# The last ten groups of a first layer's last pass by seven quarter products instead of eight

## The chip, the cores and the metric

The kernel runs on one core of a Trainium2 chip. The metric is device time in microseconds (us) of one execution; three runs of the kernel before were timed, and one more was profiled.

## What is computed

Attention over 4 x 8 heads with a threshold under the row maximum, then two feed-forward layers on 2304 tokens of 512 values. Cut to what matters here:

```
x = attention(q, k, v, tau)                      # 2304 x 512
x = (sigmoid(x @ w_gate) * (x @ w_val)) @ w_out  # first layer, 1536 hidden
h = x @ w2_in                                    # second layer, 2048 hidden
g = where(h >= 1, h, where(h <= -1, 0, (h + 1)**2 / 4))
out = g @ w2_out
```

## The kernel before, in words

The inputs of the layers are held as float32, and each product of two float32 matrices is made of three matmuls of rounded pieces: high times high, high times low, low times high. ScalarE writes the high piece (a copy to the rounded type), VectorE the low one (source minus high). The tiles `win_0` and `win_1` hold the high and the low pieces of the weights in the second layer, `wout_0` to `wout_3` both pieces of output weights, `xflat` and `xmore` those of x, `hh` and `hl` those of the hidden values.

The tokens are taken in three passes of 768 (`T`), each in two halves of 384 (`HT`). The hidden values are taken in groups of 128: 12 groups per pass in the first layer (`NF[0]`), 16 in the second, two at a time, eight pairs per pass (`NQ`).

*First layer.* `hidden` does one group: for each half, `up` (L504) makes the gate and the value, four k blocks times three matmuls of 384 columns each, 48 for a group. ScalarE takes the sigmoid, VectorE multiplies, and both make the pieces of the product. Behind it `down` (L777) adds the group before to six accumulators `y`, 24 matmuls. In the gaps `conversions` (L515) turns the weights of later groups and of the second layer from 64-bit words to float32, in pieces taken eight per group step in the first pass and six later (L879), and stores them in device memory (`saved`). After each two groups of the second layer `w_sums` (L539) makes four differences of their quarters on VectorE and stores them (`tsaved`).

*Second layer.* `pair` (L708) does two groups. Their two weight blocks and two k halves make a 2 x 2 block matrix, the two halves of x and their two k halves another one. Seven products of quarters (`product`, L630: six matmuls of 384 columns, 42 in all) give what eight would give, with sums and differences of quarters of x (`x_sums`) and of the weights (`tsum`) made beforehand, and with sums of the products afterwards: ScalarE copies two of them (`s1`, `u2`), VectorE adds five times from PSUM (L715). Products use two PSUM banks in turn. Behind the products stand the 36 output matmuls of the pair before (`down_pair`).

The weight pieces of the next pair go into the same `win_0` and `win_1`: each region is free when the product that reads it last is done. 512 columns (blocks 0 and 1) serve the first two products, 1024 columns (the differences, from `tsum`) the third to sixth, 256 columns the seventh.

*The order.* Each engine runs its instructions in the order in which they are written. In the second layer everything that is not a product, its copies and its additions goes through a list: `due` enters it with a due time on a written-out scale, a first and a last slot and a cost on VectorE or ScalarE, and `fill` (L669) is called three times per pair and writes what is due and fits. The costs, due times and slots are numbers in the program.

## Time and profile before

| what | us |
|---|---|
| median of three runs | 1105.14 (1104.94 to 1107.15) |
| the profiled execution | 1104.5 |
| its span, first to last instruction | 1102.7 |
| TensorE busy | 1082.9 (98%) |
| VectorE busy | 844.2 (77%) |
| ScalarE busy | 614.8 (56%) |

Attention ends at about 290 us. The first layer's passes run to 707 us, the second layer from there to the end. A busy TensorE is not TensorE at its peak, since matmuls are pipelined: the start of each is what counts.

### The profile page before, as it was taken

What the parts mean: (1) busy time and instruction counts of PE and PEld (TensorE: products, weight loads), DVE (VectorE), ACT (ScalarE), POOL (GpSimd) and SP (SyncE); (2) the same over time, 40 slices, a digit from 0 to 9 for tenths busy, and PEclk for the clock granted to TensorE, in tenths of its full rate; (3) what the DMA queues carried; (4) which work ended last, traced back from release to release, by engine and by line L of the source; (5) the groups of instructions that cost most, each with busy time, mean ns of one, the idle gap of its engine ahead of it and who ended that gap; (6) DMA issues with size and microseconds to landing.
All of it is one profiled execution on the core that took longest, in us unless ns stands there. A gap on an engine that the chain in (4) does not pass through costs nothing.

```text
span 1102.7 us, 18536 instructions
## 1 busy us (share of the span) xinstructions
PE 1082.9 (98%) x6996; PEld 933.3 (85%) x6996; DVE 844.2 (77%) x1489; ACT 614.8 (56%) x1000; POOL 152.7 (14%) x315
## 2 busy tenths in 40 slices
PE   8999999999999999999999999999999999999998
PEld 6666666667899999999999999988898898888887
DVE  7999999997999988767686744576767767776663
ACT  6888888886343444333353322565566655665653
POOL 4556666552000000000000000000000000000000
PEclk9999999999999999999999999999999999999999
DMA  5344344413855566545654342223232423233301
GB/s 157 70 100 79 93 99 100 102 34 103 277 199 179 176 214 218 175 150 175 202 172 151 116 153 77 77 77 125 86 114 75 165 105 115 96 134 115 115 20 58
DMA packets 65146, 139.17 MB, mean 126 GB/s; under 512 B 9616, under 2 KB 35872, under 8 KB 65056
## 3 DMA queue, kind: packets, MB, share of 16 engines
q1 hardware_dynamic: 64912, 137.98, 39.2%
q8 instruction: 55, 0.90, 0.3%
q14 instruction: 35, 0.29, 0.1%
q10 hardware_dynamic: 144, 0.00, 0.0%
HBM read 111.15 MB, written 26.81 MB: 125 GB/s over the span
## 4 chain that ended last, share of the span: by engine, by line
PE 85%; ACT 7%; DVE 5%; issue 3%; POOL 0%; DVEq 0%; POOLq 0%; ACTq 0%
PE y L771 14%; PE pu L636 14%; PE y L789 13%; PE pgv L511 9%; PE pgv L512 9%; PE pgv L513 9%; PE av L338 6%; PE w L253 5%; PE w L306 4%; ACT ex L274 2%; PE w L249 1%; ACT sqs L645 1%; ACT sqs L646 1%; ACT hh L654 1%; DVE s L262 1%
## 5 line engine op out<-in xcount | busy, mean ns | idle before, releaser
L511 PE MATMUL pgv<-xflat,win 128*128 128x384 f32 x560 | 187.9, 336 | 3.0 <-DVE act L571 1.8
L512 PE MATMUL pgv<-xflat,win 128*128 128x384 f32 x560 | 187.9, 335 | 0.0
L513 PE MATMUL pgv<-xflat,win 128*128 128x384 f32 x560 | 187.8, 335 | 0.0
L771 PE MATMUL y<-wout,hh 128*128 128x512 f32 x576 | 184.1, 394 | 0.0
L789 PE MATMUL y<-hh,wout 128*128 128x512 f32 (+1 forms) x576 | 146.5, 336 | 0.0
L771 PEld LDWEIGHTS y<-wout,hh 128*128 128x128 f32 x576 | 108.2, 188 | 24.5
L262 DVE TENSOR_SCALAR_CACHE_REDUCE s<-w,nscale 128x576 f32<-128x576 f32 x144 | 112.2, 812 | 9.7 <-PE w L253 7.6
L571 DVE TENSOR_TENSOR act<-pgv,act 128x384 f32<-128x384 f32 x70 | 38.8, 554 | 105.2 <-PE pgv L513 104.9
L572 ACT ACTIVATE hh<-act 128x384 fp32r<-128x384 f32 x72 | 38.0, 528 | 141.7 <-DVE act L571 141.7
L771 PE MATMUL y<-wout,hl 128*128 128x512 f32 x288 | 113.6, 395 | 0.0
L282 DVE SCALAR_TENSOR_TENSOR p<-s,mx,ex 128x576 f32<-128x576 f32 x144 | 111.6, 807 | 0.0
L511 PEld LDWEIGHTS pgv<-xflat,win 128*128 128x128 f32 x560 | 105.6, 188 | 5.0 <-DVE act L571 2.1
L274 ACT ACTIVATE ex<-s,mx 128x576 f32<-128x576 f32 x144 | 104.3, 766 | 6.3 <-DVE s L262 5.9
L789 PEld LDWEIGHTS y<-hh,wout 128*128 128x128 f32 x576 | 98.1, 188 | 11.3
L512 PEld LDWEIGHTS pgv<-xflat,win 128*128 128x128 f32 x560 | 105.5, 188 | 1.6
L636 PE MATMUL pu<-xflat,win 128*128 128x384 f32 x576 | 105.2, 337 | 1.4 <-DVE sqs L715 1.1
L567 ACT ACTIVATE act<-pgv 128x384 f32<-128x384 f32 x70 | 34.2, 489 | 128.7 <-PE pgv L513 128.6
L513 PEld LDWEIGHTS pgv<-xflat,win 128*128 128x128 f32 x560 | 105.7, 189 | 0.0
L636 PEld LDWEIGHTS pu<-xflat,win 128*128 128x128 f32 x576 | 100.6, 188 | 3.1 <-DVE sqs L715 2.0
L789 PE MATMUL y<-hl,wout 128*128 128x512 f32 (+1 forms) x288 | 97.1, 337 | 0.0
L265 POOL TENSOR_SCALAR mx<-mx,tau_b 128x1 f32<-128x1 f32 x144 | 87.4, 607 | 54.7 <-DVE s L262 54.5
L253 PE MATMUL w<-qk 64*128 64x288 f32 x512 | 88.2, 430 | 2.9 <-DVE s L262 2.9
(153 smaller groups left out, 1866.0 us busy)
## 6 DMA issues: line engine op xcount, KB each, us to landing
words<-in_moe_w_out_dram SPq DMA_DIRECT2D x26, 512.0 KB
wmore<-saved SPq DMA_DIRECT2D x24, 512.0 KB
tsum<-tsaved SPq DMA_DIRECT2D x24, 512.0 KB
w<-saved SPq DMA_DIRECT2D x24, 512.0 KB
w<-saved SPq DMA_DIRECT2D x14, 768.0 KB
words<-in_moe_w_in_dram SPq DMA_DIRECT2D x16, 512.0 KB
saved<-w SPq DMA_DIRECT2D x16, 512.0 KB
wmore<-saved SPq DMA_DIRECT2D x10, 768.0 KB
```

The source lines that it names most:

```text
L253: nc.tensor.matmul(w[:, s, :HS], t[es, 0, u * P : u * P + P], t[es, 1, c], start=True, stop=True)
L262: nc.vector.tensor_scalar(t[:, e], w[:, :, :HS], nscale, None, op0=ALU.mult, op1=ALU.min, accum_out=mx[:, 0, e : e + 1])
L265: nc.gpsimd.tensor_scalar(mx[:, 1, e : e + 1], mx[:, 0, e : e + 1], tau_b, None, op0=ALU.add)
L274: nc.scalar.activation(ex[:, e], t[:, e], AF.Exp, scale=-1.0, bias=mx[:, 0, e : e + 1])
L282: nc.vector.scalar_tensor_tensor(pr[:, e], t[:, e].rearrange("p a b -> p (a b)"), mx[:, 1, e : e + 1], ex[:, e].rearrange("p a b -> p (a b ...
L338: nc.tensor.matmul(av[e * D : e * D + D, :n], vs[p % 3][:, e, c], rt[r][:, e, c] if c < nf else rl[r], start=c == 0, stop=c == nf,)
L511: nc.tensor.matmul(ps, ih[:, i, kk], xh[:, kk, c], start=(kk == 0), stop=False)
L512: nc.tensor.matmul(ps, ih[:, i, kk], xl[:, kk, c], start=False, stop=False)
L513: nc.tensor.matmul(ps, il[:, i, kk], xh[:, kk, c], start=False, stop=(kk == KD - 1))
L636: nc.tensor.matmul(ps[bank], l[:, k], r[:, k], start=bool(new) and k == m == 0, stop=k == HK - 1 and m == 2, skip_group_check=True,)
L771: nc.tensor.matmul(y[b], l[:, ts_], r, start=first and m == 0, stop=last and m == 2)
L789: nc.tensor.matmul(at(y, a, b), l[:, ds_], r[:, c], start=new and m == 0, stop=last and m == 2, skip_group_check=True,)
```

## The change

Ten of the twelve groups in the first layer's last pass are taken by seven products as well. Two groups make two stages: a gate stage (even g: both groups' gates, then their sigmoids) and a value stage (odd g: both groups' values, times the sigmoids, then the pieces). `pair` becomes `stage(g)`: g from 0 to 9 is first layer, from 10 on second layer (q = g - 10). Behind stage 0 stand no output matmuls; behind stages 1 to 9 the 24 of one group each; behind stage 10 the 48 of the last two groups.

The weight differences are made one stage ahead on VectorE (`w_sums` with `due_w`): for the ten stages from the loaded weights, never stored; for the second layer in its first pass, then stored and loaded in its later passes. The conversions take eight pieces per step in both passes and end with the second. The x pieces of the first layer are laid out so that three of the seven operands of the stages are pieces that the ordinary groups had; four are made anew.

```diff
-            def w_sums(j):
-
-                b11, b21, b12, b22 = (w[:, i * HC : (i + 1) * HC] for w in w2s for i in range(2))
...
+            def w_sums(g):
+
+                b11, b21, b12, b22 = quarters(g)
+                t2, t3, t1, t4 = (tsum[:, i * HC : (i + 1) * HC] for i in range(4))
+                q = g - N1
+
+                def step(n, o, a, b):
+                    nc.vector.tensor_tensor(o, a, b, op=ALU.subtract)
+                    if n == 3 and q >= 0:
+                        nc.sync.dma_start(out=tsaved[q], in_=tsum)
...
-            LEN = lambda q: 11 if q == 0 else 15
-            start = lambda q: sum(LEN(i) for i in range(q))
+            lens = [7] + [11] * (N1 - 1) + [15] * (NPASS * NQ + 1)
+            start = lambda g: sum(lens[:g])
...
+            def due_w(g):
+                at = start(g)
+                if g < N1 + NQ:
+                    due(4 * g - 3, 4 * g - 1, [(at - 3 + 0.1 * i, 0.4, 0, True, w) for i, w in enumerate(w_sums(g))])
...
+                if q < 0:
+                    if g % 2 == 0:
+                        sig = lambda x: nc.scalar.activation(x, x, AF.Sigmoid)
+                        due(4 * g + 3, 4 * g + 7, [(at + 0.5 + i, 0, 0.9, True, lambda x=x: sig(x)) for i, x in enumerate(c)])
                     else:
...
+                        for i in range(2):
+                            h = hts[0, NPASS - 1, F0 + 2 * n + i] = h_tiles()
+                            when = ((-3.5, -3.4, -2.9), (-3.3, -2, 0.5))[i]
+                            a, *b = gated_steps(c[i], cs[n][i], h, [at + x for x in when])
+                            due(4 * g + 3, 4 * g + 3, [a])
+                            due(4 * g + 3, 4 * g + 7, b)
...
+            def gated_steps(c, s, h, at):
+
+                return [
+                    (at[0], 0.92, 0, False, lambda: nc.vector.tensor_tensor(c, c, s, op=ALU.mult)),
+                    (at[1], 0, 0.82, False, lambda: nc.scalar.activation(h[0], c, AF.Copy)),
+                    (at[2], 0.92, 0, False, lambda: nc.vector.tensor_tensor(h[1], c, f32(h[0]), op=ALU.subtract)),
+                ]
...
-                ops = 8 if order[s][1] == 0 else 6
...
+                work = itertools.islice(conv, 8)
+                if s == NB - 2:
...
+                elif s == NB - 1:
+                    work = (w[4]() for i in (2, 4, 6) for w in split_steps(0, 0, 0, *x_split(0, i)))
...
+                if s == NB - 1:
+                    due_x(0, (3,))
                     due_w(0)
                     fill(-1, 4.4, 4.4)
...
-            for q in range(NPASS * NQ):
-                pair(q)
...
+            for g in range(N1 + NPASS * NQ):
+                q = g - N1
+                if g % 2 == 0 and g + 2 < N1:
+                    for x in order[NB + g + 2 : NB + g + 4]:
+                        load_step(*x)
...
+                stage(g)
+                if q <= 0 < g:
+                    for x in order[NB - 2 + g : NB - 1 + g] if q else order[-2:]:
+                        down(*x[1:], y)
```

The matmuls on `pgv` (gate and value by `up`) go from 1680 to 1200, those on `pu` (quarter products) from 1008 to 1428; the output matmuls stay 1728. VectorE has 98 instructions more, ScalarE 24.

The three places below are all on VectorE. In the names, `pu` and `pgv` are PSUM banks with products, `act`, `high0` the copies and sums of products, `tsum` the four differences of weights, `win_1` the low and `win_0` the high weight pieces, `w32` and `wmore` loaded weights, `rb`, `raw_1`, `sqs`, `vals` the sums for one group each, `ssum` and `raw_0` sums for x.

First place: inside the last pass of the first layer. Before, one ordinary group step on VectorE:

```order
L571 TENSOR_TENSOR act_7157<-pgv_7159,act_7157 128x384
L192 TENSOR_TENSOR win_1_3510<-w32_0_82,win_1_3510 128x1024
L574 TENSOR_TENSOR hl_7156<-act_7157,hh_7155 128x384
L192 TENSOR_TENSOR wout_2_3512<-w32_0_82,wout_2_3512 128x512
L691 TENSOR_TENSOR xmore_7050<-xall_72,xmore_7050 128x768
L571 TENSOR_TENSOR act_7194<-pgv_7196,act_7194 128x384
L574 TENSOR_TENSOR hl_7156<-act_7194,hh_7155 128x384
```

Now, from the last addition of value stage 3 to the first one of gate stage 4:

```order
L749 TENSOR_TENSOR raw_1_88<-pu_6633,act_6636 128x384
L717 TENSOR_TENSOR wout_3_6159<-wmore_3619,wout_3_6159 128x512
L826 TENSOR_TENSOR rb_73<-rb_73,vals_6161 128x768
L826 TENSOR_TENSOR raw_1_88<-raw_1_88,vals_6161 128x768
L828 TENSOR_TENSOR hl_6693<-rb_73,hh_6692 128x768
L621 TENSOR_TENSOR tsum_6160<-w32_1_83 128x256
L621 TENSOR_TENSOR tsum_6160<-w32_0_82,tsum_6160 128x256
L717 TENSOR_TENSOR win_1_3510<-w32_0_82,win_0_89 128x512
L717 TENSOR_TENSOR win_1_3510<-tsum_6160,win_0_89 128x1024
L749 TENSOR_TENSOR sqs_6162<-pu_6734,act_6735 128x384
```

The low weight piece for the next stage's first product (512 columns) stands behind two multiplications, a low piece of h and two differences, where an ordinary step has two operations on the hidden values and two weight pieces.

Second place: the entry to the stages. Before, from the last ordinary group to the first addition of the first pair:

```order
L571 TENSOR_TENSOR act_7288<-pgv_7290,act_7288 128x384
L574 TENSOR_TENSOR hl_7256<-act_7288,hh_7255 128x384
L691 TENSOR_TENSOR win_1_3510<-wmore_3619,win_0_89 128x512
L691 TENSOR_TENSOR win_1_3510<-tsum_7053,win_0_89 128x1024
L691 TENSOR_TENSOR win_1_3510<-wmore_3619,win_0_89 128x256
L691 TENSOR_TENSOR xflat_86<-xall_72,xflat_86 128x768
L691 TENSOR_TENSOR xflat_86<-ssum_7051,xflat_86 128x768
L715 TENSOR_TENSOR sqs_7055<-pu_7355,act_7356 128x384
```

Now, from the last ordinary group to the first addition of stage 0:

```order
L562 TENSOR_TENSOR act_6303<-pgv_6305,act_6303 128x384
L565 TENSOR_TENSOR hl_6269<-act_6303,hh_6268 128x384
L717 TENSOR_TENSOR xmore_6157<-ssum_6158,xmore_6157 128x768
L717 TENSOR_TENSOR xmore_6157<-raw_0_87,xmore_6157 128x768
L621 TENSOR_TENSOR tsum_6160<-w32_2_84,w32_1_83 128x256
L621 TENSOR_TENSOR tsum_6160<-w32_2_84,tsum_6160 128x256
L621 TENSOR_TENSOR tsum_6160<-w32_2_84 128x256
L621 TENSOR_TENSOR tsum_6160<-w32_1_83,tsum_6160 128x256
L717 TENSOR_TENSOR win_1_3510<-w32_1_83,win_0_89 128x512
L717 TENSOR_TENSOR win_1_3510<-tsum_6160,win_0_89 128x1024
L717 TENSOR_TENSOR win_1_3510<-w32_2_84,win_0_89 128x256
L749 TENSOR_TENSOR sqs_6162<-pu_6376,act_6377 128x384
```

Four differences, which were loaded from memory before, now stand ahead of the first low weight piece.

Third place: the exit. There was no such place before. Now, behind the last addition of stage 9, to the piece behind the first addition of stage 10:

```order
L717 TENSOR_TENSOR wout_0_90<-wmore_3619,wout_0_90 128x512
L717 TENSOR_TENSOR wout_2_3512<-w32_0_82,wout_2_3512 128x512
L717 TENSOR_TENSOR win_1_3510<-w32_1_83,win_0_89 128x512
L717 TENSOR_TENSOR xflat_86<-xall_72,xflat_86 128x768
L826 TENSOR_TENSOR rb_73<-rb_73,sqs_6162 128x768
L826 TENSOR_TENSOR raw_1_88<-raw_1_88,sqs_6162 128x768
L828 TENSOR_TENSOR hl_7276<-rb_73,hh_7275 128x768
L621 TENSOR_TENSOR tsum_6160<-w32_1_83,tsum_6160 128x256
L717 TENSOR_TENSOR xflat_86<-xall_72,xflat_86 128x768
L717 TENSOR_TENSOR win_1_3510<-tsum_6160,win_0_89 128x1024
L749 TENSOR_TENSOR sqs_6162<-pu_7318,act_7319 128x384
L717 TENSOR_TENSOR xmore_6157<-ssum_6158,xmore_6157 128x768
```

The low pieces of x for the second and third product of stage 10 stand behind the multiplications of stage 9.

## Rows read from the trace of the kernel before

**Rows 1.** Busy time by stretch, TensorE to GpSimd, granted clock, DMA share, GB/s.

```profile
200.00:300.00 100.00, 93.24 (x787) 70.88 (x784) 90.02 (x183) 67.54 (x119) 38.35 (x69) 0.98 0.44 129
290.00:440.00 150.00, 150.00 (x865) 143.54 (x864) 137.16 (x179) 64.28 (x115) 0.00 (x0) 1.00 0.59 198
581.89:707.03 125.14, 125.14 (x722) 119.76 (x722) 66.35 (x100) 38.85 (x67) 0.00 (x0) 1.00 0.30 104
707.03:764.57 57.54, 55.33 (x289) 49.99 (x289) 41.48 (x61) 36.14 (x57) 0.00 (x0) 1.00 0.31 110
764.57:867.51 102.94, 102.77 (x505) 91.05 (x504) 74.87 (x103) 65.59 (x95) 0.00 (x0) 1.00 0.30 108
```

**Rows 2.** Timeline of TensorE: start, duration, engine, line, operation, of two group steps.

```profile
579.81 0.33 PE L511 MATMUL pgv<-xflat,win 128*128 128x384 f32 x1
...
581.89 0.39 PE L789 MATMUL y<-hh,wout 128*128 128x512 f32 x1
...
707.03 0.39 PE L789 MATMUL y<-hh,wout 128*128 128x512 f32 x1
...
711.22 1.03 PE L636 MATMUL pu<-xmore,win 128*128 128x384 f32 x5
```

**Rows 3.** Chain of waits: start, time, what, of the second layer's second pair.

```profile
749.08 8.31 PE y L771 x36
757.38 7.35 PE pu L636 x42
```

**Rows 4.** Timeline of TensorE, the waits at the change-over.

```profile
726.56 0.62 PE L636 MATMUL pu<-xmore,win 128*128 128x384 f32 x2 [1.53 <-ACT act L730]
...
742.93 1.34 PE L636 MATMUL pu<-xmore,win 128*128 128x384 f32 x6 [0.34 <-ACT act L730]
744.61 0.61 PE L636 MATMUL pu<-xflat,win 128*128 128x384 f32 x2 [0.34 <-DVE sqs L715]
```

**Rows 5.** Timelines of TensorE and VectorE at a stage's end, second layer.

```profile
827.75 0.39 PE L771 MATMUL y<-wout,hh 128*128 128x512 f32 x1
...
827.95 0.56 DVE L715 TENSOR_TENSOR rb<-pu,act 128x384 f32<-128x384 f32 x1 [0.48 <-PE pu L636]
828.42 0.95 DVE L691 TENSOR_TENSOR xmore<-xall,xmore 128x768 fp32r<-128x768 f32 x1
829.29 0.95 DVE L691 TENSOR_TENSOR xmore<-ssum,xmore 128x768 fp32r<-128x768 f32 x1
830.15 0.68 DVE L691 TENSOR_TENSOR wout<-wmore,wout 128x512 fp32r<-128x512 f32 x1
830.76 1.22 DVE L691 TENSOR_TENSOR win<-tsum,win 128x1024 fp32r<-128x1024 f32 x1
831.89 0.42 DVE L691 TENSOR_TENSOR win<-w,win 128x256 fp32r<-128x256 f32 x1
```

**Rows 6.** Timeline of VectorE, the differences of one pair.

```profile
643.25 0.42 DVE L545 TENSOR_TENSOR high<-w,w 128x256 f32<-128x256 f32 x1
643.70 0.42 DVE L545 TENSOR_TENSOR high<-w,high 128x256 f32<-128x256 f32 x1
644.04 0.42 DVE L545 TENSOR_TENSOR high<-w 128x256 f32<-128x256 f32 x1
```

**Rows 7.** Timelines of ScalarE and VectorE, the last group and a pair.

```profile
708.44 0.56 DVE L574 TENSOR_TENSOR hl<-act,hh 128x384 fp32r<-128x384 f32 x1 [0.59 <-ACT hh L572]
...
708.32 0.62 ACT L690 ACTIVATE win<-wmore 128x512 fp32r<-128x512 f32 x1
708.84 1.05 ACT L690 ACTIVATE win<-tsum 128x1024 fp32r<-128x1024 f32 x1
...
818.66 0.85 ACT L654 ACTIVATE hh<-vals 128x768 fp32r<-128x768 f32 x1 [1.03 <-DVE vals L652]
...
819.54 0.96 DVE L655 TENSOR_TENSOR hl<-vals,hh 128x768 fp32r<-128x768 f32 x1 [0.91 <-ACT hh L654]
```

**Rows 8.** Waits of the DMA queue from 300 us: total us, times, longest.

```profile
SPq L622 <- DMA tsum<-tsaved: 40.4, 17, 3.7
```

212 lines of the change are left out of this document (117 added, 95 removed).

## The prediction

> **What bounds the kernel now.** I read the busy time by stretch first. From 290 us on TensorE is the bound: it is busy 150.00 of 150.00 us from 290 to 440 and 125.14 of 125.14 in the last ten group steps of the first layer; the change-over to the second layer (707.03 to 764.57) has gaps, 55.33 of 57.54 [rows 1]. So I next read the starts of TensorE's instructions, because a start cannot be hidden by a modelled end. Twelve gate/value matmuls of 384 columns start in 2.08 us, from 579.81 to 581.89, 0.173 us each; the 24 output matmuls of a group take 4.19 us, 707.03 to 711.22 [rows 2]. A second-layer stage takes 7.35 us for its 42 product matmuls and 8.31 for 36 output matmuls [rows 3]. The change-over has three waits, 1.53, 0.34 and 0.34 us of idle by the profile, and the matmuls after one start more slowly, six in 1.34 us: five intervals of 0.20 instead of 0.173, 0.13 us more per wait [rows 4]. The length of the stretch gives the whole loss: two times 4.19, four times 7.28 and two times 8.31 make 54.1 of 57.5 us, 3.4 lost, of which 0.3 are the 0.07 by which each 42 take longer than 42 times 0.173: 3.1 are waits.
>
> **What is removed.** Ten group steps had 48 gate/value matmuls each, 480; ten stages have 42, 420. Sixty matmuls fewer at 0.173 are **-10.4 us**, all on the path, since TensorE has no gap there. The old change-over goes too: **-3.1 us**.
>
> **What is added.** Ninety-eight VectorE and 24 ScalarE instructions, and a tight order. A group step has 12.5 us of TensorE for 66.35/10 = 6.6 us of VectorE [rows 1]. A new stage has 7.28 + 4.19 = 11.5 us, but two stages (gate, then value of two groups) give VectorE ten additions at 0.56, eight subtractions at 0.42, two low weight pieces each of 512, 1024 and 256 columns at 0.68, 1.22 and 0.42, two output pieces at 0.68, two gate multiplications and two low pieces of h at 0.95: 18.8 us of 23.0 [rows 5, 6]. That fits as a sum; whether it fits in place is the question, since the weight tiles are single: the low piece for the next stage's first product must be written after this stage's second product and before the next stage's third matmul.
>
> The durations for the walk: VectorE starts 0.20 us after TensorE's end (827.75, 827.95); from start to start an addition takes 0.47, 768 columns 0.87, 512 columns 0.61, 1024 columns 1.13 [rows 5]; a 256-column subtraction 0.34, 0.45 when the next one needs it [rows 6]; the last one before a waiting engine counts in full. ScalarE's copy of 768 columns is 0.85, of 1024 columns 1.05 [rows 7]. A hand-over between them is 0.03 to 0.04 (a copy ends at 819.51, VectorE's piece on it starts at 819.54 [rows 7]), and each wait of TensorE at 0.13 more for the restart [rows 4]. The order is that of VectorE's rows, three pieces of which stand above.
>
> *Value stage to gate stage* (3 to 4, 5 to 6, 7 to 8). After the last product VectorE does addition, output piece, two multiplications, the low piece of h (which waits for ScalarE's copy of the first product, 0.13), two subtractions, then the low weight piece: 0.20 + 0.47 + 0.61 + 1.74 + 0.13 + 0.87 + 0.68 + 0.68 + 0.04 = 5.4 us. TensorE has 4.19 of output matmuls and two first matmuls, 4.54. Wait 0.9, with restart 1.0; three times **3.1**. The gate stages have no multiplications and pass with about 1.6 us to spare: nothing. At stage 8 to 9, where three operations on x stand among them, 0.9.
>
> *Stage 1 to 2.* Here the weight piece stands before the multiplications, and the subtractions behind them; the 1024-column piece of the differences (ScalarE 1.05, then VectorE 1.22) comes last: 0.20 + 0.47 + 1.22 + 1.74 + 0.13 + 0.87 + 0.76 + 0.04 + 1.05 + 0.04 + 1.22 = 7.7 us against 4.19 + 2.08 + 0.35 = 6.6 to the third matmul of the third product. **1.3** with restart.
>
> *Entry.* After the last ordinary group the low piece of h starts 1.41 us after 707.03 (708.44), and ScalarE's next copy at 1.29 [rows 7]. Two x pieces follow (the first waits for its copy, 1.29 + 0.84 + 0.04, and ends at 3.04, the second at 3.91), four subtractions (1.45), the weight piece (0.68): 6.0 us, needed at 4.54; 1.6 with restart. Two later pieces in stage 0 cost 0.6. No output matmuls stand behind stage 0: 0.20 + 0.47 + 1.02 + 0.68 = 2.4 against 0.35, 2.2 with restart. Sum **4.4**.
>
> *Exit, stage 9 to 10.* Output pieces and weight piece (1.83), a low piece of x (0.87), two multiplications, h, a subtraction and then the second x piece: 0.67 + 1.83 + 0.87 + 1.74 + 0.13 + 0.87 + 0.34 + 0.95 = 7.4 against 4.19 + 1.04 + 0.17 = 5.4: 2.2 with restart. The third x piece stands behind the addition that waits for the second product: 0.20 + 0.47 + 0.95 against 0.17, 1.7 with restart and the piece ahead. Four more x pieces stand ahead of the next addition: 0.3 and 1.0. Sum **5.3**. The first pairs of the second layer keep 1.2 of the old change-over's waits (ScalarE still copies the finished first layer ahead of a product's copy).
>
> Sum of waits: 4.4 + 1.3 + 3.1 + 0.9 + 5.3 + 1.2 = **16.2**. Net: 16.2 - 10.4 - 3.1 = +2.7, against the profiled 1104.5 us: 1107.2. The median of the runs shown is 1105.14, 0.6 above that execution; on its scale 1107.8. This is the forecast, **1107.8**: slower by a little.
>
> **Edits at nothing.** The weight differences of the second layer move from the first layer's steps into the second layer's first pass, 1.4 us of VectorE per stage, seven times; before, VectorE was busy 74.87 of 102.94 us there, 11.4 of 15.7 per stage [rows 1], so 12.9 fit; without this cover a stage would grow by at most 1.4. The conversions now run eight pieces per step in the second pass, where it was six; the first pass ran eight, larger ones, with VectorE at 137.16 of 150.00 and no idle TensorE [rows 1]. Of the DMAs, a store of the differences takes the place of a load; the next subtraction waits for its landing. The queue waited at most 3.7 us for a load of that size to land [rows 8]; the shortest distance by the walk is about 6 us.
>
> **A rule that speaks against the change.** The granted clock is 1.00, 2.4 GHz, in the stretch with the 1.53 us wait, and 0.98 between 200 and 300 us where TensorE was idle for 6.8 of 100 us [rows 1, 4]. The Trainium skill (TensorE: Matmul & The Clock Gate, Why this matters for your kernels) warns that idle gaps between bursts of matmuls bring the lower clock back; by that rule the longest new waits could cost twice, and the trace agrees only so far as the mean fell in the stretch with most idle time.
>
> **Bounds.** Without restarts (some 13 times 0.13) and with no hand-overs, the waits are 14.2: net +0.7, 1105.8 on the median's scale. With the 0.07 per stage on top at ten new stages and waits a quarter longer, 20.3 + 0.7 - 13.5: +7.5, 1112.6. I take the sum because each term is nearest to a row of the same operation and size.
>
> **Rivals.**
> 1. *The budget decides, not the place* (not slower). If VectorE, at 18.8 of 23.0 us, catches up within each stage, the 3.1 + 1.3 + 0.9 in the middle do not occur: -2.6, 1102.5. Decides where the low weight piece is written 0.9 us earlier than in my walk. For it: the second layer's stages run without waits at 11.4 of 15.7. Against it: there 8.31 us of output matmuls follow the products, here 4.19. 0.17.
> 2. *VectorE's instructions do not overlap.* An instruction that needs the one before starts 0.11 later (0.45 against 0.34) [rows 6]. If that holds for most of the eight in each of eight chains, 64 times 0.08 = 5 us more: 1112.8. Decides if start to start is the full duration. The Trainium skill (VectorE: DVE Perf Modes, The DRAIN you can't avoid) says that a held next operation starts only when the pipe of the one before is empty; the trace agrees for the dependent subtractions and shows no more. Against it: most rows here depend on other engines. 0.11.
> 3. *The clock.* The stretch at 0.98 has 2 us in 100 missing [rows 1]; two such at entry and exit: +4, 1111.7. Against: 1.00 through the present change-over. 0.03.
> 4. *The second pass becomes VectorE's.* The first pass leaves VectorE 12.84 of 150.00 us [rows 1], 1.1 per step of 12.5; where the second pass needs 0.2 more than a step, in twelve steps, +2.4, 1110. Against: its pieces are smaller. 0.03.
>
> **Numbers.** The forecast has 0.66, spread from 1105.8 to 1110. About 0.2%, 2.2 us, is what a measurement of this kernel can tell from no change: below 1107.35 lie 0.31 of it, above 0.35. Faster 0.17 (rival 1), same 0.31, slower 0.35 + 0.11 + 0.03 + 0.03 = 0.52. The range 1103.0 to 1111.5 leaves out rival 1 and a little at the top.
>
> **What would show it.** In the profile after, "pu" should have 1428 matmuls and "pgv" 1200 beside the 48 early ones; TensorE's waits should be on the low pieces of win at the third matmul of stages 0, 1, 4, 6 and 8 (1.6, 2.2, then 1.0 each), on the 1024-column piece in stage 2, and on x pieces in stage 10 (2.2 and 1.7), all released by VectorE. Ten waits below 0.3 would make the prediction wrong on the fast side; a granted clock below 1.00 after 580 us, or waits in every gate stage, on the slow side.

## The result, and the profile after

The changed kernel takes 1112.43 us (median of 6 runs, 1110.72 to 1114.39), the kernel before 1105.66 in runs on the same chip (6 runs, 1104.94 to 1107.15). The ratio is 1.0064, interval 1.0054 to 1.0075: slower by 6.8 us. I forecast slower by 2.7, and the time lies 0.9 above the range. The profiled execution took 1112.1 us, span 1110.3; the page's busy times, which answer to those shown of before:

```profile
PE 1081.2 (97%) x6936; PEld 925.7 (83%) x6936; DVE 899.3 (81%) x1587; ACT 633.4 (57%) x1024; POOL 152.1 (14%) x315
...
PEclk9999999999999999999999999899999999999999
...
L662 PE MATMUL pu<-xflat,win 128*128 128x384 f32 x816 | 163.3, 340 | 8.2 <-DVE win L717 4.6
...
L518 PE MATMUL pgv<-xflat,win 128*128 128x384 f32 x400 | 134.2, 336 | 3.0 <-DVE act L562 1.8
...
L662 PE MATMUL pu<-xmore,win 128*128 128x384 f32 x612 | 126.3, 340 | 4.5 <-ACT act L776 2.8
```

The change did what it says: "pu" has 816 + 612 = 1428 matmuls and "pgv" three times 400, the counts named ahead. TensorE's busy time fell (1082.9 before, 1081.2 now) and the time rose, so the time went into idle time: the two "pu" lines show 8.2 + 4.5 = 12.7 us of it. In which stretch it lies, the same windows as in [rows 1] tell, with the second pass beside them (busy time by stretch, columns as there):

```profile
290.00:440.00 150.00, 150.00 (x864) 143.24 (x863) 141.45 (x182) 64.38 (x117) 0.00 (x0) 1.00 0.60 202
440.00:582.00 142.00, 142.00 (x819) 136.09 (x818) 115.13 (x163) 57.20 (x103) 0.00 (x0) 1.00 0.56 194
581.89:707.03 125.14, 118.49 (x665) 109.67 (x664) 93.52 (x162) 52.74 (x84) 0.00 (x0) 1.00 0.15 49
707.03:764.57 57.54, 54.31 (x264) 48.02 (x262) 44.62 (x71) 35.59 (x54) 0.00 (x0) 0.94 0.26 92
764.57:867.51 102.94, 101.31 (x502) 90.29 (x503) 78.30 (x121) 62.62 (x92) 0.00 (x0) 1.00 0.34 119
```

The passes before 582 us still have no idle TensorE. The ten stages do, and the change-over has a granted clock of 0.94. TensorE's timeline (start, duration, engine, line, operation, in brackets the idle time before it and who ended it) has the waits:

```profile
589.08 2.03 PE L662 MATMUL pu<-xflat,win 128*128 128x384 f32 x10 [1.40 <-DVE win L717]
...
592.68 1.14 PE L662 MATMUL pu<-xflat,win 128*128 128x384 f32 x5 [0.19 <-DVE xflat L717]
...
597.60 0.62 PE L662 MATMUL pu<-xflat,win 128*128 128x384 f32 x2 [0.65 <-DVE sqs L749]
...
599.20 2.02 PE L662 MATMUL pu<-xflat,win 128*128 128x384 f32 x10 [0.98 <-DVE win L717]
...
613.30 0.62 PE L662 MATMUL pu<-xmore,win 128*128 128x384 f32 x2 [0.53 <-ACT act L776]
...
636.12 2.01 PE L662 MATMUL pu<-xflat,win 128*128 128x384 f32 x10 [0.72 <-DVE win L717]
...
707.84 1.20 PE L662 MATMUL pu<-xflat,win 128*128 128x384 f32 x6
...
709.61 0.44 PE L662 MATMUL pu<-xflat,win 128*128 128x384 f32 x1 [0.56 <-ACT xflat L716]
711.08 1.14 PE L662 MATMUL pu<-xflat,win 128*128 128x384 f32 x5 [1.03 <-DVE xflat L717]
712.49 0.44 PE L662 MATMUL pu<-xmore,win 128*128 128x384 f32 x1 [0.27 <-ACT xmore L716]
713.97 1.97 PE L662 MATMUL pu<-xmore,win 128*128 128x384 f32 x5 [1.04 <-DVE xmore L717]
715.74 2.12 PE L662 MATMUL pu<-xflat,win 128*128 128x384 f32 x6
717.66 2.12 PE L662 MATMUL pu<-xmore,win 128*128 128x384 f32 x6
...
721.91 0.39 PE L856 MATMUL y<-hh,wout 128*128 128x512 f32 x1
```

The low piece of the weights at the third matmul holds TensorE in stage 0 (589.08), stage 1 (599.20) and stage 4 (636.12; the two like it are at 660 and 684), as the prediction has it. Elsewhere six matmuls take 1.2 to 1.3 us; the groups at 713.97 (five), 715.74 and 717.66 take about 2 us with no wait among them. The granted clock there (the column behind GpSimd's), in windows of 1 us and one of 0.25:

```profile
709.00:710.00 1.00, 0.43 (x2) 0.19 (x1) 1.00 (x2) 0.56 (x1) 0.00 (x0) 1.00 0.00 0
...
713.00:714.00 1.00, 0.03 (x1) 0.03 (x1) 1.00 (x3) 1.00 (x2) 0.00 (x0) 0.64 0.99 303
713.25:713.50 0.25, 0.00 (x0) 0.00 (x0) 0.25 (x1) 0.25 (x2) 0.00 (x0) 0.57 1.08 393
714.00:715.00 1.00, 1.00 (x3) 1.00 (x4) 1.00 (x2) 1.00 (x3) 0.00 (x0) 0.50 0.99 381
...
719.00:720.00 1.00, 1.00 (x5) 1.00 (x4) 0.18 (x1) 0.00 (x0) 0.00 (x0) 0.50 0.02 8
720.00:721.00 1.00, 1.00 (x7) 1.00 (x6) 0.37 (x1) 0.00 (x0) 0.00 (x0) 0.94 0.00 0
```

TensorE stood still 0.56, 1.03 and 0.27 us, and 0.35 us into a fourth wait of 1.04 us, at 713.3, the clock fell from 1.00 to 0.50, 1.2 GHz. It stayed there until 720 us.

**The ledger**, from starts of TensorE's instructions. The output group that starts at 581.89 in [rows 2] starts at 582.98 after: of the 7.6 us between the two profiled executions 1.1 arise ahead of the stages, and 6.5 are to be explained (6.8 by the medians). Of the 1.1, 0.8 are there when VectorE first reads attention's scores (6.80 before, 7.57 after) and 0.3 arise at 416 us; through the second pass the lag stays at 1.08. Kernels that leave all this code alone reach the same group between 581.15 and 586.01 in their profiled executions (e1 to e7, e9, e13, described below), so 1.1 is no more than executions differ by.

| place | measured | forecast |
|---|---|---|
| sixty matmuls, old change-over's waits | -13.5 | -13.5 |
| ten stages, 587.17 to 707.84, against 10 x 7.28 + 9 x 4.19 = 110.5 | +10.2 | +9.7 |
| exit stage, 707.84 to 721.91, against 7.28 | +6.8 | +5.3 |
| first pairs of the second layer | +0.9 | +1.2 |
| end of the second layer's first pass | +2.3 | 0 |
| sum | +6.7 | +2.7 |

(The sum is 0.2 above 6.5, since the lag also shrinks by 0.45 us between 778 and 841 us and grows by 0.2 behind 860.) Two rows carry the miss: the exit, 1.5, and a place that the prediction priced at nothing. There the lag behind the kernel before grows from 5.1 us, at the pair that starts at 841.21, to 7.4 at the next one, and then stays within 0.2. The pair takes 18.16 us of TensorE (841.21 to 859.37), before 15.88. The rows of that place, from the timelines of VectorE, ScalarE and TensorE:

```profile
826.64 0.95 DVE L599 TENSOR_TENSOR xall<-xall 128x768 f32<-128x768 f32 x1
...
833.10 0.56 DVE L749 TENSOR_TENSOR rb<-pu,act 128x384 f32<-128x384 f32 x1 [0.49 <-PE pu L662]
...
839.98 0.95 DVE L717 TENSOR_TENSOR xflat<-xall,xflat 128x768 fp32r<-128x768 f32 x1
840.85 0.95 DVE L678 SCALAR_TENSOR_TENSOR vals<-vals,sqs 128x768 f32<-128x768 f32 x1
841.84 0.85 ACT L680 ACTIVATE hh<-vals 128x768 fp32r<-128x768 f32 x1 [4.59 <-DVE vals L678]
843.84 0.47 ACT L776 ACTIVATE act<-pu 128x384 f32<-128x384 f32 x1
844.36 1.31 PE L662 MATMUL pu<-xmore,win 128*128 128x384 f32 x6 [0.91 <-ACT act L776]
855.30 0.50 PE L838 MATMUL y<-wout,hl 128*128 128x512 f32 x1 [0.49 <-DVE hl L681]
```

Between the last addition of the pair before (833.10) and the instruction that finishes its hidden values (840.85, L678) VectorE has six low pieces of the next pass's x, the last at 839.98, and rests nowhere. ScalarE's queue holds the copy of h, which waits 4.59 us for L678, and behind it the copy of a product (843.84), for which TensorE waits.

### The profile page after: what moved, and what is told of

It reads as the page before. It is cut to its first block, busy times and chain, and to the rows that moved or that the text cites. A ratio compares the mean times of both kernels' runs of the same rounds, so it can differ in the third digit from the quotient of the medians.

```text
span 1110.3 us, 18522 instructions
## 1 busy us (share of the span) xinstructions
PE 1081.2 (97%) x6936; PEld 925.7 (83%) x6936; DVE 899.3 (81%) x1587; ACT 633.4 (57%) x1024; POOL 152.1 (14%) x315
## 4 chain that ended last, share of the span: by engine, by line
PE 82%; DVE 8%; ACT 7%; issue 3%; POOL 0%; DVEq 0%; ACTq 0%; POOLq 0%
PE pu L662 21%; PE y L838 15%; PE y L856 11%; PE pgv L518 6%; PE pgv L519 6%; PE pgv L520 6%; PE av L338 6%; PE w L253 5%; PE w L306 4%; ACT ex L274 2%; PE w L249 1%; DVE win L717 1%; DVE wout L717 1%; DVE tsum L621 1%; DVE s L262 1%
## 5 line engine op out<-in xcount | busy, mean ns | idle before, releaser
L662 PE MATMUL pu<-xflat,win 128*128 128x384 f32 x816 | 163.3, 340 | 8.2 <-DVE win L717 4.6
L662 PEld LDWEIGHTS pu<-xflat,win 128*128 128x128 f32 x816 | 144.3, 189 | 15.9 <-DVE win L717 6.4
L518 PE MATMUL pgv<-xflat,win 128*128 128x384 f32 x400 | 134.2, 336 | 3.0 <-DVE act L562 1.8
L519 PE MATMUL pgv<-xflat,win 128*128 128x384 f32 x400 | 134.2, 335 | 0.0
L520 PE MATMUL pgv<-xflat,win 128*128 128x384 f32 x400 | 134.1, 335 | 0.0
L662 PE MATMUL pu<-xmore,win 128*128 128x384 f32 x612 | 126.3, 340 | 4.5 <-ACT act L776 2.8
L662 PEld LDWEIGHTS pu<-xmore,win 128*128 128x128 f32 x612 | 108.8, 190 | 7.9 <-ACT act L776 5.3
L856 PEld LDWEIGHTS y<-hh,wout 128*128 128x128 f32 x576 | 98.5, 189 | 11.4
L563 ACT ACTIVATE hh<-act 128x384 fp32r<-128x384 f32 x52 | 27.4, 528 | 107.4 <-DVE act L562 107.4
L314 ACT ACTIVATE r<-w 128x1024 f32<-128x1024 f32 x64 | 65.1, 1018 | 29.9 <-PE w L306 29.5
L518 PEld LDWEIGHTS pgv<-xflat,win 128*128 128x128 f32 x400 | 75.2, 188 | 4.7 <-DVE act L562 2.1
L253 PEld LDWEIGHTS w<-qk 64*128 64x128 f32 x512 | 49.3, 187 | 34.5 <-DVE s L262 20.0
```

The lines of the kernel that those rows point to most:

```text
L253: nc.tensor.matmul(w[:, s, :HS], t[es, 0, u * P : u * P + P], t[es, 1, c], start=True, stop=True)
L518: nc.tensor.matmul(ps, ih[:, i, kk], xh, start=(kk == 0), stop=False)
L519: nc.tensor.matmul(ps, ih[:, i, kk], xl, start=False, stop=False)
L520: nc.tensor.matmul(ps, il[:, i, kk], xh, start=False, stop=(kk == KD - 1))
L662: nc.tensor.matmul(ps[bank], l[:, k], r[:, k], start=bool(new) and k == m == 0, stop=k == HK - 1 and m == 2, skip_group_check=True,)
L856: nc.tensor.matmul(at(y, a, b), l[:, ds_], r[:, c], start=new and m == 0, stop=last and m == 2, skip_group_check=True,)
```

## The experiments

Each kernel is compared with the kernel before, run on the same chip; a ratio stands with its 95% interval, and e1 to e16 are the kernels by the start of their labels. "After" is the changed kernel; a difference from it is one of medians, 1112.43 less the median named. The code cuts show the lines that matter, not every line of an edit.

**What costs 2.3 us at the end of the pass?** Theory: the four differences of each second-layer pair, now in this pass, displace other work. Rival: the conversions' new places. In the first kernel the differences of pairs 5 to 8 are loaded from other stored numbers instead of being formed; its second layer computes with these. In the second, everything is computed, but the four differences of x for the next pass are due two stages earlier.

```diff
-                if g < N1 + NQ:
+                if g < N1 + 4:
...
-                nc.sync.dma_start(out=tsum, in_=tsaved[q % NQ])
+                nc.sync.dma_start(out=tsum, in_=tsaved[q % NQ] if q % NQ < 4 else saved[1, 2 * (q % NQ)])
```

> Changed kernel, but the weight differences of the second layer's fifth to eighth pair are not made on VectorE in the first pass: numbers of the same size are loaded in their place, as the kernel before did (they are weights and not differences, so the products of these pairs are others). Theory: these sixteen short instructions push the last x difference of the next pass, and with it one x piece of 0.87 us, behind the other work of the last stage of the first pass; the waits of about 1.1 us and 0.9 us around 844 and 855 us go, and the time falls by 1.9 to 2.3 us, to about 1110.3. Rival: the first pass ends late for another reason (loads of the differences for the second pass, the stores, the freed buffers): the waits stay and the time stays within 0.5 us of the changed kernel's 1112.4.

```diff
-                if j == NQ - 4 and o < NPASS:
+                if j == NQ - (6 if q >= 0 else 4) and o < NPASS:
```

> Changed kernel, computing the same, with the four x differences of the next pass of the second layer spread from the third stage of a pass on instead of from the fifth; nothing is taken from VectorE. Theory (order, not load): the x piece is in its old place again, the waits at the end of the first pass go as in the run before, 1.5 to 2.2 us off, about 1110.4. Rival (load): VectorE has too much work over the stretch whatever its order, and 0.5 us or less comes back.

Measured: 1110.27, ratio 1.0041 [1.0026, 1.0055], and 1110.24, 1.0043 [1.0028, 1.0058]. Both are 2.2 below 1112.43. The intervals still touch that of after, 1.0054 to 1.0075; the timelines show the same size, since the pair that took 18.16 us takes 16.04 in the first and 16.00 in the second. In the second all differences are still formed. One of the six x pieces now stands at 830.79, ahead of the last additions, so that only five stand between them and L678, which starts 1.22 us ahead of the pair (842.89) and not 0.36. The product that waited 0.91 us starts without a wait (timelines of VectorE and TensorE):

```profile
830.79 0.96 DVE L717 TENSOR_TENSOR xflat<-xall,xflat 128x768 fp32r<-128x768 f32 x1
...
841.67 0.94 DVE L678 SCALAR_TENSOR_TENSOR vals<-vals,sqs 128x768 f32<-128x768 f32 x1
...
845.18 1.31 PE L662 MATMUL pu<-xmore,win 128*128 128x384 f32 x6
```

So the differences cost by moving one piece of 0.87 us into a place where two queues stand behind it, not by their sum. The difference of x at 826.64 is the link by the order of the rows: in after it stands where the other two kernels have an output-weight piece or nothing, and the pieces behind it come later.

**Is the exit's 1.5 the clock?** 21 repeated matmuls fill the exit's waits (its first products in pass 1 are summed with repeats, so the output is of other numbers):

```diff
+                for n in range(pre):
+                    nc.tensor.matmul(ps[bank], *first, start=bool(new) and n == 0, stop=False, skip_group_check=True)
...
-                product(1, ps)
+                product(1, ps, *((4, 7) if q == 0 else ()))
...
-                product(2, ps)
+                product(2, ps, *((3, 7) if q == 0 else ()))
```

> Changed kernel with 21 matmuls (3.6 us) put into TensorE's four waits of the first stage of the second layer (3.9 us): products already made are added once more, so the sums of that stage are others. The waits stay as long as they were, TensorE only has work in them. Theory: the granted clock fell to 0.50 because TensorE stood still there; with the waits filled it stays at 1.00 through 707 to 722 us, the matmuls behind keep 0.173 us each, and 2.5 to 3 us come off, about 1109.7. Rival: the clock falls for another reason (what all engines and the transfers do at once), then it is 0.50 from about 713 us as before and the time is the changed kernel's 1112.4 or more.

Measured: 1111.56, 1.0056 [1.0041, 1.0071]. Windows and TensorE's timeline:

```profile
600.00:601.00 1.00, 1.00 (x4) 1.00 (x4) 0.52 (x1) 1.00 (x3) 0.00 (x0) 0.50 0.00 0
...
713.00:714.00 1.00, 1.00 (x8) 0.93 (x7) 1.00 (x3) 1.00 (x3) 0.00 (x0) 1.00 0.49 143
```

```profile
708.87 1.20 PE L667 MATMUL pu<-xflat,win 128*128 128x384 f32 x6
...
719.27 1.33 PE L667 MATMUL pu<-xflat,win 128*128 128x384 f32 x6 [0.81 <-DVE high L754]
...
721.49 0.39 PE L861 MATMUL y<-hh,wout 128*128 128x512 f32 x1
```

With TensorE busy the clock stays at 1.00 through the exit, and the exit stage takes 12.62 us (708.87 to 721.49) instead of 14.07. Up to the end of the fourth wait both kernels are alike (6.15 us from the stage's start, 6.13 in after), so the repeats didn't lengthen the waits and the 1.45 come behind them. What is left is 5.3 over 7.28, and it lies where the prediction had it: 2.08, 1.82, 0.25 and 1.18, forecast 2.2, 1.7, 0.3 and 1.0. The slow pace itself took 2.9 more than 2.4 GHz would have; only 1.45 of it counted, since at full pace TensorE waits for VectorE (719.27). The median fell by 0.9 only, which is within the intervals, so the 1.45 stand on the two traces. The first window shows one reason: in this execution the clock is at 0.50 in stage 1 too, in code that this kernel doesn't touch.

**Can the exit be reordered?** The next two put the first three x pieces and the first weight piece of the second layer ahead of the exit's other work, and the multiplications and output weights behind (the second line pair is that of the second kernel). In the first, two output-weight pieces are split after the load that replaces their source, so the ninth and tenth groups' output products use other weights.

```diff
-                    due(first, last, split_steps(start(g) + i - 1, 0.84, 0.7, *x_split(o, i)))
+                    at = start(g - 1) + 5 + 0.1 * i if o == 1 and i < 3 else start(g) + i - 1
+                    due(first, last, split_steps(at, 0.84, 0.7, *x_split(o, i)))
...
-                            when = ((-3.5, -3.4, -2.9), (-3.3, -2, 0.5))[i]
+                            when = ((-3.5, -3.4, -2.9), (-3.3, -2, 0.5))[i] if g < N1 - 1 else ((1.05, 1.06, 1.3), (1.1, 1.2, 5.4))[i]
```

> Changed kernel, computing the same, with another order on VectorE and ScalarE at the step from the first layer's last stage to the second layer's first: the first three x pieces and the first weight piece ahead of the two gate multiplications, and the two output-weight pieces behind that stage. Theory: VectorE has the same work, but what TensorE needs first comes first: the four waits of 3.9 us shrink to 1.4 us or less, the clock does not fall, and 4.5 to 5.5 us come off, about 1107.5. Rival (VectorE's load decides, not its order): the waits only move by a product or two, to the third and fourth, with the same sum, the clock falls a little later, and under 1 us comes off.

> Changed kernel, computing the same, with another order on VectorE and ScalarE at the step from the first layer's last stage to the second layer's first: three x pieces and the first weight piece ahead of the two gate multiplications, the two output-weight pieces (1.2 us of VectorE) behind the remaining x pieces. The run with the waits filled showed that VectorE sets the end of this stage: from 704.3 to 718.7 us it never rests, and the slow clock only used up time in which TensorE would have waited. Theory (order): from 707.8 to 721.9 us the stage lasts 14.1 us where its 42 matmuls need 7.3; with the pieces first it loses 3 us instead of 6.8, 3 to 4.5 us off, about 1108.5. Rival (load): only the 1.2 us that were moved behind come off, 1111.2, and the waits move to the third to sixth product.

Measured: 1120.15, 1.013 [1.0112, 1.0149], and 1115.65, 1.0087 [1.0067, 1.0107]. Both are misses. In the first the product waits shrink to 0.20, 0.51, 0.21 and 0.40, but the low piece of h, put behind, then holds the output products for 3.70 us; in the second for 3.09, and its clock still falls:

```profile
724.22 0.80 PE L859 MATMUL y<-hl,wout 128*128 128x512 f32 x1 [3.09 <-DVE hl L831]
```

The order was not the exit's only limit: from 709 to 715 us of after's exit VectorE is busy 5.67 of 6 us. TensorE needs other work over it.

**Can the waits of the middle be ordered away?** The first weight piece goes ahead of the multiplications.

```diff
-                    ((-1, 4 * g - 3, 4 * g - 1, 0.6), (1.3, 4 * g - 1, 4 * g + 1, 0.32), (1, 4 * g - 1, 4 * g - 1, 1.1))
+                    ((-3.6 if g <= N1 else -1, 4 * g - 3, 4 * g - 1, 0.6), (1.3, 4 * g - 1, 4 * g + 1, 0.32), (1, 4 * g - 1, 4 * g - 1, 1.1))
...
+                fill(4 * g + 2, 0.85 if q < -1 else 0, 0, small=True)
```

> Changed kernel, computing the same, with another order on VectorE inside the ten stages: the low part of the first weight piece (0.60 us) ahead of the four differences and of the gate multiplications, up to two short instructions between the third and fourth product of a stage, and the four x differences of the next pass one stage apart. Theory (order): TensorE's waits for that low part, 0.88 us at 636, 660 and 684 us and 1.25 us at 599 us, go; 2.5 to 3.5 us off, about 1109.4. Rival (load): the next piece, over the differences, is late instead, the waits come back at the third product of the same stages, and under 1 us comes off.

Measured: 1116.37, 1.0098 [1.0071, 1.0124]. The three waits of 0.88 at the first product are gone, and from the start of stage 4 to that of stage 5 it is still 12.47 us (12.48 in after): the wait is now on the 1024-column piece two products later (TensorE's timeline):

```profile
594.62 1.31 PE L662 MATMUL pu<-xmore,win 128*128 128x384 f32 x6 [1.96 <-ACT act L776]
...
640.92 0.97 PE L662 MATMUL pu<-xmore,win 128*128 128x384 f32 x4 [0.27 <-DVE win L717]
```

The 3.9 us that this kernel is slower than after are not lost, by its profiled execution (the slowest of the four), in the ten stages, which take 120.26 us (120.67 in after), but at the exit, where the piece goes ahead too: its products and output products take 27.66 us (710.46 to 738.12) instead of 22.45, with a wait of 3.09 us for the low piece of h, as in e5.

**What are the stage differences worth?** The 40 differences of the ten stages are left out (their weights are split in place, so the first layer's last pass uses other numbers).

```diff
-                if g < N1 + NQ:
+                if N1 <= g < N1 + NQ:
...
-                    src, a = ((quarters(g)[3], 2 * HC), (tsum, 3 * HC))[i - 1]
+                    src, a = ((quarters(g)[3], 2 * HC), (tsum if g >= N1 else w32[0, NPASS - 1, F0 + 2 * (g // 2)][:, : 4 * HC], 3 * HC))[i - 1]
```

> Changed kernel without the forty weight differences of the ten stages: the weights themselves are split in their place, so the gate and value sums are others. VectorE has 13.6 us less to do (40 x 0.34). Theory: the entry's waits for the first weight piece (1.56 and 1.25 us) and the three value-to-gate waits (0.88 us each) are this work's place in VectorE's queue; they go, and some of the exit, 5 to 6.5 us off, about 1106.5. Rival: the waits come from what else stands there (gate multiplications, x pieces, output weights), and under 2.5 us comes off.

Measured: 1108.02, 1.0027 [1.0014, 1.0041]. The ten stages take 113.0 us instead of 120.67, 7.7 less, and the exit with its output products gives 3.5 of it back (25.92 us instead of 22.45, with waits of 2.19, 1.04 and 3.10 us). Three quarters of the 10.2 lost in the stages hang on 13.6 us of subtractions, 40 at 0.34.

**The entry.** The first four differences go into the last ordinary group, between the first and the second of the three x operands that are split there.

```diff
-                if g < N1 + NQ:
+                if 0 < g < N1 + NQ:
...
-                    work = (w[4]() for i in (2, 4, 6) for w in split_steps(0, 0, 0, *x_split(0, i)))
+                    parts = [[w[4] for w in split_steps(0, 0, 0, *x_split(0, i))] for i in (2, 4, 6)]
+                    work = (w() for w in (*parts[0], *w_sums(0), *parts[1], *parts[2]))
```

> Changed kernel, computing the same, with the four differences of the first stage made in the last step of the old kind, between that step's two halves, where VectorE rested for 1.3 to 3.4 us at a time, and not between that step and the stage. Theory: the wait of 1.56 us at 589 us goes and nothing takes its place, 1.3 to 1.9 us off, about 1110.8. Rival: the differences wait for the second group's weights there and hold up the step's own multiplication, or the third product waits instead: under 0.6 us comes off, or it is slower.

Measured: 1109.05, 1.003 [1.0018, 1.0043], 3.4 below after. TensorE's timeline has twelve matmuls in one run where two and a wait of 1.40 stood:

```profile
586.69 2.52 PE L662 MATMUL pu<-xflat,win 128*128 128x384 f32 x12
...
595.10 0.62 PE L662 MATMUL pu<-xflat,win 128*128 128x384 f32 x2 [0.65 <-DVE sqs L749]
```

Stage 0 takes 8.41 us (586.69 to 595.10) instead of 10.43. By the two traces the ten stages take 2.13 us less and the exit stage 0.62 less, together 2.7. The rest of the 3.4 would fit the clock at the entry, which costs 1.5 where it falls. That it fell in after's unprofiled runs isn't shown; all that speaks for it is their mean granted clock, 0.994 in three of five, where the profiled execution, in which it didn't fall there, has 0.995.

**Two of them together**, the earlier differences of x and the entry:

> Changed kernel, computing the same, with the two edits that each took time off: the second layer's x differences two stages earlier (2.2 us) and the first stage's weight differences in the last step of the old kind (3.4 us). They lie 250 us apart. Theory: they add, 1106.8, give or take 0.7. Rival: what is won at the entry is given back at the exit, as 3.5 of 7.7 us were when all stage differences were left out, and under 4 us comes off, 1108.4 or more.

Measured: 1107.64, 1.0026 [1.0016, 1.0037]; 4.8 below after, where the parts gave 2.2 and 3.4.

**A cover at the exit.** One output group of the middle is held back, so that two stand between stage 9 and the exit. In the first of these kernels (and in e11 and e12, built on it) the eighth output group is computed twice and the tenth not at all, since it has `g >= 4` where the line shown, the second kernel's, has `4 <= g < N1`.

```diff
-                    for x in order[NB - 2 + g : NB - 1 + g] if q else order[-2:]:
+                    a = NB - 2 + g - (4 <= g < N1)
+                    for x in order[a : a + (0 if g == 4 else 2 if g >= N1 - 1 else 1)]:
```

> Changed kernel, computing the same, with one group of output matmuls (18 matmuls or 4.2 us of TensorE) moved: none stands between the fifth and the sixth stage, each later one comes one stage later, and so two stand between the tenth stage and the second layer's first. Between the fifth and sixth stage the differences go into an earlier gap. Theory: at the exit VectorE has 14 us of work from 704 us on whatever its order, and TensorE too little to do beside it (the stage takes 14.1 us for 7.3 us of matmuls); 4.2 us more cover there take most of the 6.8 us loss away, the clock does not fall, and the place that gives its cover up pays 1 to 1.5 us: 2.5 to 4.5 us off, about 1108.9. Rival: the waits at the exit come from an order (a piece that stands behind another), so the matmuls end later but wait as long, and nothing or 1 us comes off.

> Changed kernel, computing the same, with one group of output matmuls taken from between the fifth and sixth stage and two put at the exit, as in the run before that had a wrong group there. Theory (amount): VectorE's chain from 702 us on starts 2.3 us earlier than in the changed kernel and is as long, so the exit ends 2 us earlier, the waits that are left (0.5, 1.1 and 0.9 us in the third to fifth product) stay, the 2.2 us wait at the output matmuls goes, and the clock stays up: 2 to 3 us below the changed kernel, 1109.4 to 1110.4. Rival (order): one piece behind another decides, and with the cover nearly all 6.8 us come back: 1107 or less.

Measured: 1113.47, 1.0074 [1.0061, 1.0087] (a wait of 2.00 us for output weights), and with the tenth group 1111.13, 1.0051 [1.0034, 1.0068]. In the latter the exit's products take 10.30 us instead of 14.07 and the clock stays up (windows):

```profile
600.00:601.00 1.00, 1.00 (x4) 1.00 (x4) 0.47 (x1) 1.00 (x3) 0.00 (x0) 0.50 0.00 0
...
712.00:714.00 2.00, 1.19 (x6) 0.61 (x4) 1.15 (x2) 2.00 (x5) 0.00 (x0) 1.00 0.97 367
```

Of these 3.8 us, 1.7 are lost where the group was taken away, in stages 4 and 5 (635.87 to 653.17, 17.30 us for two stages of products that took 8.29 + 7.33), and 1.5 at the entry, whose clock fell in this execution.

**All three** (e11; e14 with the tenth group), and two variants: in e12 the differences of x stand one stage apart and up to two short instructions between the third and fourth product of stages 3, 5 and 7; in e15 the exit's output weights come later.

```diff
+                fill(4 * g + 2, 0.85 if g == 4 or g in (3, 5, 7) else 0, 0, small=True)
...
+                        if g == N1 - 1:
+                            first, end = 4 * g + 6, 4 * g + 6
```

> Changed kernel, computing the same, with all three edits: x differences earlier, entry differences earlier, and two groups of output matmuls at the exit. Theory: they add, since the exit now has the cover that the earlier start of it needs: 1103.2, between 1102.3 and 1104.5, below the kernel before at 1105.3. Rival: the exit stays bound by VectorE and takes what the others give, 1105 or more.

> The same three edits, and the last two differences of a value stage go between its third and fourth product, so that the first weight piece of the gate stage behind it comes 0.7 us sooner; the low part of the second group's hidden values goes behind the pieces, and the x differences of the next pass come one stage apart. Theory: the three waits of 0.88 us go and each costs 0.2 to 0.3 us between the products: 1.2 to 2 us less than the run with three edits, about 1101.6. Rival: as in the run with the first weight piece early, the piece over the differences is late in its place, and it is the same as the run with three edits within 0.5 us.

> Changed kernel, computing the same, with the three edits (x differences of the second layer earlier, entry differences earlier, two output groups at the exit, the right ones). Theory: 2.2 us below the run with the wrong groups (1107.9), 1105.7, between 1104.8 and 1106.5, the time of the kernel before. Rival: the wait of 2.2 us is taken over by the low part of the ninth group's hidden values, and it stays at 1107.5 or more.

> The three edits, and the two output-weight pieces of the last two groups (1.2 us of VectorE, 1.0 us of ScalarE) go behind the fourth product of the second layer's first stage, with the load that takes their place behind them. Theory (amount of work ahead of the x pieces): the waits of 0.5, 1.1 and 0.9 us in the third to fifth product of that stage go for the most part, 1.2 to 2.2 us less than the run with three edits: 1103.8, between 1103 and 1105, below the kernel before. Rival: VectorE is late with the adds instead, the sixth and seventh product wait, and less than 0.5 us comes off.

Measured: 1107.93, 1.0031 [1.002, 1.0043]; 1108.48, 1.0034 [1.0021, 1.0047]; then, with the tenth group, 1106.61, 1.001 [0.9999, 1.0021]; and with the output weights of the exit later 1107.01, 1.0016 [1.0006, 1.0027]. Neither variant gains. In the third the exit's products still take 10.30 us, though VectorE rests 1.79 us ahead of its first addition there (710.41): under the longer cover it may be the order again. So the third and fourth x piece go ahead of the exit too, and, beside them, two short instructions between two products of stage 1:

```diff
-                    last = 4 * g - 1 if i < 2 else 4 * g + 1
-                    due(first, last, split_steps(start(g) + i - 1, 0.84, 0.7, *x_split(o, i)))
+                    last = 4 * g - 1 if i < (4 if o == 1 else 2) else 4 * g + 1
+                    due(first, last, split_steps(start(g) + (0.1 * i if o == 1 and i in (2, 3) else i - 1), 0.84, 0.7, *x_split(o, i)))
...
+                if g in (1, 4):
+                    fill(4 * g + 2, 0.85, 0, small=True)
```

> The run with three edits (right groups), computing the same, with the third and fourth x piece of the second layer's first stage ahead of that stage's first copy, where the two output groups now cover them, and the last two differences of the third stage between two products of the second. Theory: the waits in the third to fifth product at the exit shrink from 2.8 to under 1 us, the 1.8 us at the third stage's third product to 0.8: 2.5 to 3 us below the run with three edits (1106.6), 1103.8, below the kernel before at 1105.2. Rival: the pieces over the differences come later for it and the third product waits for them: under 1 us comes off, 1105.6 or more.

Measured: **1104.13 (11 runs, 1102.55 to 1106.09) against 1105.42, ratio 0.9987 [0.9978, 0.9996]**: below both kernels, the kernel before by 1.3 us, with an interval that ends just below 1. TensorE's timeline at the exit:

```profile
706.95 2.24 PE L662 MATMUL pu<-xflat,win 128*128 128x384 f32 x12
...
711.67 1.34 PE L662 MATMUL pu<-xmore,win 128*128 128x384 f32 x6 [0.39 <-ACT act L785]
713.32 1.31 PE L662 MATMUL pu<-xflat,win 128*128 128x384 f32 x6 [0.30 <-DVE high L749]
```

The exit's products take 8.56 us (706.95 to 715.51) where e14 has 10.30. The other edit has its share: from the start of stage 2 to its output products it is 8.25 us, 9.26 in e14. From the first stage to here it is 127.9 us where after has 134.7. And from the output group at 582 to 583 us to the end of the profiled execution it is 519.2 us, against 520.8 before and 527.3 after, so the 1.3 us don't come from the code ahead.

## Why the prediction had the direction right and was 4 us short

The prediction had the kernel slower, as it is, but by 2.7 us, and 6.8 were measured. Two of its steps failed: it put the second layer's differences at nothing, and it left the clock out of the exit. Its own upper bound, 1112.6, holds the time; the range was drawn 1.1 below that bound.

- **Removed, -13.5: right as far as seen.** 1428 and 1200 matmuls, and no idle TensorE from 290 to 582 us.
- **The walk of the waits: right in place and size, in part wrong in releaser.** Entry 1.56 and 0.36 (forecast 1.6, 0.6); stage 0 to 1 0.82 + 1.25 = 2.07 (2.2); 1 to 2 0.70 + 0.53 = 1.23 (1.3); the three value-to-gate waits 0.88 each (1.0); 8 to 9 0.80 (0.9), each with its restart. Together 8.7 of the 10.2 lost in the stages; the other 1.5 are small waits and the 0.07 per 42 matmuls, ten times, that only the bounds counted. So 10.2 against 9.7 is closer than the walk: its waits came out 1.0 smaller than forecast, and losses left out of the sum filled their place. The forecast had all of them released by VectorE's low pieces of weights and x; but 0.82 of the 2.07 at stage 1 and 0.61 of the 0.80 at stage 9 are behind additions, 0.70 of the 1.23 at stage 2 behind a copy on ScalarE (613.30), and 0.73 and 0.54 at the exit behind ScalarE's high pieces of x (709.61, 712.49). Exit 0.73 + 1.30 = 2.03 (2.2) and 0.54 + 1.31 = 1.85 (1.7), 3.9 of its 6.8; the slow pace is the other 2.9. (The four terms of the exit add up to 5.2, where the prediction writes 5.3.)
- **"Edits at nothing", the second layer's differences: the first step that failed**, 2.3 us. The price, 11.4 + 1.4 of 15.7 us of VectorE per stage, was an average over the pass. In its last stages VectorE also prepares the next pass: ahead of the last pair it works from 833.10 to 841.80 without a rest. The four differences pushed one x piece into that stretch. Forming the differences of x earlier, which takes it out again, gives 2.2 back with all the work still done (e2). The paragraph that bounded this at "at most 1.4" per stage was never carried into the sum.
- **The clock, rival 3, held at 0.03: the second.** The mechanism was as told there, one drop at the exit worth 1.45 by the traces (rival: 2); a drop at the entry, 1.5, comes in some executions. The walk itself put two waits of 2.2 and 1.7 us next to each other; the argument against it, 1.00 through the old change-over, rested on one long wait, 1.53 us, with the next, 0.34, 16 us behind it [rows 1, 4]. The rule that the prediction quoted (the Trainium skill, TensorE: Matmul & The Clock Gate, Why this matters for your kernels), that gaps between bursts bring the lower clock back, agrees with the 0.50 in after's windows; here the fall came with short waits close together. The slow pace also took the place of the exit's last two terms, 0.3 and 1.0: TensorE at half pace no longer waits for VectorE.
- **Rival 1, the budget decides: fell.** No wait of the middle is missing. **Rival 2, no overlap: fell**; independent subtractions start 0.34 apart in the stages as before. VectorE's timeline:

```profile
587.33 0.42 DVE L621 TENSOR_TENSOR tsum<-w,tsum 128x256 f32<-128x256 f32 x1
587.67 0.42 DVE L621 TENSOR_TENSOR tsum<-w 128x256 f32<-128x256 f32 x1
...
588.34 0.68 DVE L717 TENSOR_TENSOR win<-w,win 128x512 fp32r<-128x512 f32 x1
```

- **Rival 4, the second pass: fell.** TensorE is busy 142.00 of 142 us there, and VectorE 115.13; the lag behind the kernel before is 1.08 us at its start and 1.09 at its end.
- **Left open.** The 1.1 us ahead of 582 us were not tried. Why the clock falls at the entry in some executions only, no run shows. What lies between e10's 4.8 and the 5.6 of its parts is within the runs' spread.

## What to carry to other kernels

Price moved work at the place where it lands: a pass with a quarter of VectorE free on average had it busy for 8.7 us without a rest ahead of its last pair, and one more 0.87 us piece there, with two queues behind it, cost 2.2 us. Count waits together, not one by one: where several stand close, ask what the clock does afterwards. Reordering where an engine is full moved the wait (e4 to e6); moving work to where that engine rests took it away (e2, e8). Where it rests nowhere near, first put work of the waiting engine over the place, then order what the other engine does under it (e16).

## What the runs showed of the hardware

- TensorE's granted clock fell to 0.50 in the last of four waits of 0.56, 1.03, 0.27 and 1.04 us (709.05 to 713.97), none as long as the wait of 1.53 us through which it stayed at 1.00 before [rows 1, 4]. With these waits filled by repeated matmuls it stayed at 1.00.
- The same instructions with nearly the same waits (1.40, 0.19, 0.65 and 0.98 us in after, 1.41, 0.21, 0.65 and 0.99 in e3), in stages 0 and 1, leave the clock at 1.00 in after's profiled execution and at 0.50 from about 599.7 us in those of e3 and e13. There it is 14.4 us from the start of stage 1 to that of stage 2 instead of 12.9.
- Half the clock cost only half its price: of 2.9 us of slower matmuls at the exit 1.45 reached the end, because at full pace TensorE would have waited for VectorE instead.
